# Transposing q of two head pairs on VectorE in 32 by 32 blocks instead of on TensorE, with batch 1's steps respaced

## The chip, the cores and the metric

One core of a Trainium2 chip runs the whole program. The metric is the device time of one execution in microseconds (us), as the median of several. Ratios are the mean time of one kernel's fast runs over that of the other's fast runs of the same rounds, so they are not quite the ratio of the medians that stand beside them. The span of a profile is about 2.1 us shorter than the time of the same execution.

## The reference, cut to what matters

```python
kv  = np.einsum('bhsd,bhse->bhde', k, v)           # 8 batches, 8 heads, 576 rows, 64 columns
out = np.einsum('bhsd,bhde->bhse', q, kv)
rms = np.sqrt(np.mean(out * out, axis=-1, keepdims=True) + 1e-06)
x   = out / rms * g_norm                           # as 4608 rows of 512
h   = x @ w_in                                     # 512 -> 2048
y   = (h * (1 / (1 + np.exp(-1.702 * h)))) @ w_out # 2048 -> 512
```

The kernel multiplies q by kv on TensorE with the columns of q on partitions, that is, transposed (batch 1's are the four matmuls `outT<-qT,kvb` of 128x512 in its profile, 0.38 us each). It treats heads in pairs, so there are four pairs to a batch, and a pair's transposed q is a tile of 128 partitions (2 heads x 64 columns) by 576 rows. Most batches are transposed by DMA, batches 0 and 1 by TensorE.

## The kernel before

The dense part of one batch is a stage of 64 matmuls into hT (`w_in`) and a stage of 64 "steps" (`w_out`, called projection here). Work of the next batch's attention is threaded between them at chosen step numbers: `at2(n, f)` runs `f` behind step `n`. The order in which these calls are made is also the order of the instructions on each engine. Batch 1's attention runs inside the projection of batch 0:

```python
        def q(self, c):                            # class Second, batch 1
            t = ps_a.tile([P, S], F16, name="q1", tag="att")
            for j in range(NJ):                    # NJ = 6 matmuls against an identity
                nc.tensor.transpose(t[:, j * PE_ : (j + 1) * PE_],
                    qbuf[0:PE_, (c * NJ + j) * P : (c * NJ + j + 1) * P], ident[0:PE_, 0:PE_])
            s = attn.tile([P, S], F16, name="qT", tag="qT", bufs=4)
            nc.vector.tensor_copy(s, t)            # PSUM to SBUF
            self.qT[c] = s
# ... (the threading, t == 0)
            for c in range(NPAIR):
                at1(12, of(1, "pack_q", c))        # qraw -> qbuf, VectorE
                at2(9 + 3 * c, of(1, "q", c))
                at2((21, 21, 33, 33)[c], of(1, "pack_k", c))    # kraw -> kbuf, VectorE
                at2((23, 24, 42, 43)[c], of(1, "kv", c))        # TensorE; behind pairs 1 and 3 VectorE copies kvb
                o = (27, 31, 48, 52)[c]
                at2(o, of(1, "out", c))                         # TensorE, reads qT and kvb
                at2(o + 7 - c // 2, of(1, "ss", c))             # sum of squares, then Ln and Exp on ScalarE
                at2(o + 7 - c // 2, of(1, "apply", c))          # VectorE, writes x
# ... (the loads into SBUF, all on one queue, in this order)
    load_w_out(0, 4)
    early_load("q", 1, 0, NPAIR)
    load_w_out(4, 8)
    for c in (0, 2):
        early_load("k", 1, c, c + 2)
        early_load("v", 1, c, c + 2)
        load_w_out(8 + 2 * c, 12 + 2 * c)
```

The projection goes through `w_out` in quarters: steps 0 to 15 use the first, steps 16 to 31 the second, 32 to 47 the third, 48 to 63 the last.

Of the kernel before, what the change touches and what calls it, by code (L numbers as in the profile page):

```python
# [7 lines left out]
F16 = mybir.dt.float16  # L8
# [4 lines left out]
P = 128  # L13
# [3 lines left out]
def kernel(  # L17
# [10 lines left out]
    nc = tc.nc  # L28

    B, H, S, D = q.shape  # L30
# [13 lines left out]
    PE_ = 96  # L44
    NJ = S // PE_
# [5 lines left out]
    attn = ctx.enter_context(tc.tile_pool(name="attn", bufs=4))  # L51
# [19 lines left out]
    qraw = const.tile([P, NPAIR, 2 * NJ * D], F16)  # L71
# [130 lines left out]
    class Attention:  # L202
# [46 lines left out]
        def rest(self, c):  # L249
            return self.qTr[:, c % 2, (c // 2) * R : (c // 2 + 1) * R]  # L250
# [150 lines left out]
    class Second(Attention):  # L401
# [26 lines left out]
        def q(self, c):  # L428
# [8 lines left out]
            nc.vector.tensor_copy(s, t)  # L437
            self.qT[c] = s

        def rest(self, c):  # L440
            return self.qT[c][:, SM:S]

# [139 lines left out]
    for hl in range(2):  # L582
        r = slice(hl * D, (hl + 1) * D)
# [25 lines left out]
    d0 = Hidden(0)  # L609
# [32 lines left out]
    for t in range(NT):  # L642
        b = t + 1
        u1, u2 = {}, {}

        def at1(i, f, *args):
            u1.setdefault(i, []).append(lambda: f(*args))

        def at2(i, f, *args):
            u2.setdefault(i, []).append(lambda: f(*args))  # L650

        def of(b, name, *args):
            return lambda: getattr(live[b], name)(*args)

        if t == 0:
            at1(7, of(0, "out", NPAIR))
            at2(4, setattr, a0, "ss_pool", Attention.ss_pool)
            at2(4, of(0, "ss", NPAIR, True))
            at2(4, of(0, "apply", NPAIR))
            at1(8, start, 1)  # L660
            for r in krem + vrem:
                at1(8, nc.vector.memset, r[R:P], 0.0)
            for c in range(NPAIR):
                at1(12, of(1, "pack_q", c))
                at2(9 + 3 * c, of(1, "q", c))
                at2((21, 21, 33, 33)[c], of(1, "pack_k", c))
                at2((23, 24, 42, 43)[c], of(1, "kv", c))
                o = (27, 31, 48, 52)[c]
                at2(o, of(1, "out", c))
                at2(o + 7 - c // 2, of(1, "ss", c))  # L670
                at2(o + 7 - c // 2, of(1, "apply", c))
        elif b < B:
            if t == 1:
                at2(46, setattr, live[1], "ss_pool", Attention.ss_pool)
                at2(46, of(1, "out", NPAIR))
                at2(53, of(1, "ss", NPAIR))
                at2(53, of(1, "apply", NPAIR))
            f0 = 5 if t == 1 else 2
            at1(f0, casts, b)
            at1(f0, start, b)  # L680
            at1(f0, of(b, "transpose_q"))
            if t + 2 < B:
                at1(f0, load_batch, t + 2)
            for c in range(NPAIR):
                at1((10 if t == 1 else 9) + c, of(b, "kv", c))
            at2(6, nc.scalar.preload_act_table_set, "natural_log_exp_and_others")
            for j in range(J):
                at2((1, 4, 8, 11)[j], of(b, "rows", j))
            at2(7, of(b, "turn", 0))
            at2(16, of(b, "turn", 2))  # L690
            at2(27, of(b, "out", NPAIR))
            at2(36, of(b, "ss", NPAIR))
            at2(36, of(b, "apply", NPAIR))
        dense(t, u1, u2, (GROUP, 5)[t] if t < 2 else 0, t == 0, None if t else d0)
# [30 lines left out]
```

## Time and profile before

The kernel took 288.66 us (four runs, 288.12 to 289.06).

| in the profile of the kernel before | value |
|---|---|
| span | 286.0 us |
| TensorE busy | 279.8 us, 98% |
| VectorE busy | 110.9 us, 39% |
| first projection stage | 28.74 to 47.21 us, 18.47 us |
| VectorE busy in that stage | 8.69 us |

The table says that TensorE is the bound, and that VectorE has room. The lines that carry it, and how they are read, stand in the prediction below.

### The profile page before, as it was taken

To read this page: it belongs to the slowest core of one execution; us is meant where nothing else is said; L and a number is where in the kernel's file an instruction comes from. 1 tells how busy PE (TensorE), PEld (TensorE's weight loads), DVE (VectorE), ACT (ScalarE), POOL (GpSimd) and SP (SyncE) were. 2 spreads that over 40 slices of the span, in tenths; PEclk is the share of its full clock that TensorE was granted. 3 is DMA by queue.
4 is the path that set the end of the run, shared out by engine and by line. 5 is a ranking of instruction groups with operands and counts; after the bars stand their busy time and mean duration, and the time that the engine had idled before them with its cause. 6 is when DMAs were issued, how large, how long until landed. Compare 5 with 4: busy or idle time off the path is not lost.

```text
span 286.0 us, 4103 instructions
## 1 busy us (share of the span) xinstructions
PE 279.8 (98%) x1609; PEld 136.0 (48%) x1609; DVE 110.9 (39%) x219; ACT 156.1 (55%) x273; POOL 49.2 (17%) x66
## 2 busy tenths in 40 slices
PE   7899999999999999999999999999999999999994
PEld 3444544455445544554455445544554444444444
DVE  3530544627651656147603860386227400110001
ACT  2697358766575645574468536763666375017400
POOL 8831430201400140014000500032002100000000
PEclk9999999999999999999999999999999999999999
DMA  8999999999679537893699358954601230011022
GB/s 179 203 206 204 204 255 320 256 250 311 147 178 331 134 75 220 233 271 58 201 205 323 57 183 202 323 92 127 139 2 37 53 133 0 0 73 76 0 73 73
DMA packets 63589, 45.82 MB, mean 160 GB/s; under 512 B 36195, under 2 KB 60515, under 8 KB 62803
## 3 DMA queue, kind: packets, MB, share of 16 engines
q1 hardware_dynamic: 53344, 33.74, 45.4%
q0 software_dynamic: 9504, 10.86, 19.9%
q10 hardware_dynamic: 722, 0.97, 1.2%
q8 instruction: 12, 0.20, 0.3%
q14 instruction: 7, 0.05, 0.1%
HBM read 36.73 MB, written 9.44 MB: 161 GB/s over the span
## 4 chain that ended last, share of the span: by engine, by line
PE 94%; DMA 2%; POOL 2%; issue 0%; DVE 0%; POOLq 0%
PE hT L453 44%; PE o L490 42%; DMA vbuf<-in_v_dram 2%; PE kvp L221 2%; PE outR L287 2%; PE oh L520 1%; PE ss L335 1%; POOL qraw L89 1%; POOL kraw L89 1%; PE outT L255 1%; PE kvp L418 0%; PE kvp L229 0%; POOL vbuf L89 0%; PE q L431 0%; PE outT L266 0%
## 5 line engine op out<-in xcount | busy, mean ns | idle before, releaser
L490 PE MATMUL o<-w_out_sb,gT 128*128 128x512 f16 x560 | 130.7, 379 | 0.0
L462 ACT ACTIVATE gT<-hT 128x512 f16<-128x512 f32 x144 | 84.5, 599 | 77.3 <-PE hT L453 77.2
L453 PE MATMUL hT<-xT,w_in_sb 128*128 128x512 f16 x512 | 116.4, 379 | 0.0
L453 PEld LDWEIGHTS <-w_in_sb 128*128 128x128 f16 x576 | 54.9, 98 | 62.9 <-DMA w_in_sb<-in_moe_w_in_dram 1.6
L490 PEld LDWEIGHTS <-gT 128*128 128x128 f16 x560 | 53.0, 98 | 56.3 <-issue 0.2
L319 POOL TENSOR_TENSOR x<-xr,g_all 128x512 f16<-128x512 f32 x12 | 15.2, 1270 | 141.3 <-DMA vf<-in_v_dram 67.0
L500 DVE COPY osb<-o 128x512 f32<-128x512 f32 x20 | 13.8, 691 | 63.5 <-PE o L490 63.5
L298 DVE TENSOR_REDUCE sum<-sq 128x8 f32<-128x512 f16 x24 | 15.8, 678 | 18.3 <-ACT sq L295 18.3
L236 DVE CAST kvb<-kvp 64x256 f16<-64x256 f32 (+1 forms) x16 | 6.2, 388 | 43.1 <-PE kvp L229 42.0
L312 DVE TENSOR_TENSOR xr<-outR,sum 128x512 f32<-128x512 f32 x24 | 15.5, 686 | 11.1 <-ACT sum L309 11.1
L319 DVE TENSOR_TENSOR x<-xr,g_all 128x512 f16<-128x512 f32 x12 | 15.2, 1267 | 0.7
L295 ACT ACTIVATE sq<-outR 128x512 f16<-128x512 f32 x24 | 13.6, 590 | 2.0 <-PE outR L287 1.6
L275 ACT ACTIVATE sq<-outT 128x512 f16<-128x512 f32 (+1 forms) x16 | 7.7, 482 | 11.9 <-PE outT L255 10.5
L453 PE MATMUL hT<-x_rem,w_in_sb 128*128 128x512 f16 x64 | 14.0, 379 | 0.0
L500 ACT COPY osb<-o 128x512 f32<-128x512 f32 x15 | 8.7, 580 | 6.3 <-PE o L490 6.3
L308 ACT ACTIVATE sum<-sum,eps_t 128x16 f32<-128x16 f32 x12 | 3.7, 308 | 15.0 <-DVE sum L298 14.9
L337 ACT ACTIVATE ln<-ss,eps_t 128x512 f32<-128x512 f32 (+1 forms) x16 | 9.3, 584 | 2.9 <-PE ss L335 2.7
L133 DVE CAST vbuf<-vf 128x512 f16<-128x512 f32 x24 | 9.6, 459 | 2.0 <-DMA vf<-in_v_dram 2.0
L462 ACT ACT_TABLE_LOAD x8 | 10.3, 1283 | 0.1
L221 PEld LDWEIGHTS <-kbuf 128*128 128x128 f16 x96 | 7.4, 98 | 5.7
L287 PEld LDWEIGHTS <-qTd 128*128 128x128 f16 x96 | 7.4, 98 | 5.7
L221 PE MATMUL kvp<-vbuf,kbuf 128*128 128x128 f16 x96 | 9.3, 219 | 0.0
(73 smaller groups left out, 156.8 us busy)
## 6 DMA issues: line engine op xcount, KB each, us to landing
out_dram<-osb SPq DMA_DIRECT2D x6, 1024.0 KB, 4.3
qf<-in_q_dram SPq DMA_DIRECT2D x5, 1024.0 KB, 5.8
kf<-in_k_dram SPq DMA_DIRECT2D x5, 1024.0 KB, 7.8
vf<-in_v_dram SPq DMA_DIRECT2D x5, 1024.0 KB, 10.5
w_out_sb<-in_moe_w_out_dram POOLq DMA_DIRECT2D x4, 512.0 KB, 17.2
out_dram<-osb SPq DMA_DIRECT2D x6, 192.0 KB, 4.2
qf<-in_q_dram POOLq DMA_DIRECT2D x1, 1024.0 KB, 16.7
kf<-in_k_dram POOLq DMA_DIRECT2D x1, 1024.0 KB, 14.8
```

Of the source, the lines that this page charges most:

```text
L133: nc.vector.tensor_copy(out=vh[:, h, :], in_=src["v"][:, h, :])
L221: nc.tensor.matmul(t[:, c, :].rearrange("p (l d) -> p l d", l=2), kh[:, c, j, :], vh[:, 2 * c : 2 * c + 2, j * D : (j + 1) * D], start=(j ...
L287: nc.tensor.matmul(t[:, c * P : (c + 1) * P], self.qT[c][:, j * P : (j + 1) * P], self.kb[:, c, :], start=True, stop=True,)
L295: nc.scalar.activation(sq, t, AFT.Square)
L298: nc.vector.tensor_reduce(out=self.sum2[:, j % 2, :], in_=sq.rearrange("p (h d) -> p h d", h=H), op=ALU.add, axis=mybir.AxisListType.X,)
L312: nc.vector.tensor_mul(xr[:, i], self.o[j + i].rearrange("p (h d) -> p h d", h=H), s2[:, i, :].unsqueeze(2).to_broadcast([P, H, D]),)
L319: (nc.vector if i else nc.gpsimd).tensor_mul(self.x16[:, j + i, :].rearrange("p (h d) -> p h d", h=H), xr[:, i], g_all.unsqueeze(1).to_bro ...
L337: nc.scalar.activation(ln[:, 0:n], t[:, 0:n], AFT.Ln, bias=eps_t, scale=1.0 / D)
L453: nc.tensor.matmul(self.h[fo], w_in_sb[:, ko, fo * P : (fo + 1) * P], self.x[:, ko], start=(ko == 0), stop=(ko == KO - 1),)
L462: nc.scalar.activation(self.gT[:, fo, :], self.h[fo], AFT.Gelu_apprx_sigmoid)
L490: nc.tensor.matmul(os[mo], gT[:, fo, mo * P : (mo + 1) * P], w_out_sb[:, fo, :], start=(fo == 0), stop=(fo == FO - 1),)
L500: copy(osb[:, mo, :], os[mo])
```

## The change

The intent was to take work off the engine that bounds the kernel. q of pairs 2 and 3 is no longer packed, transposed by TensorE and copied out of PSUM. VectorE transposes it in 32 by 32 blocks from `qraw`, each instruction reading one group of 32 partitions and writing one, mostly another. The steps of kv, out, sums and applies are moved to suit.

```diff
+        def blocks_q(self, c, a):
+            if a == 0:
+                self.qT[c] = attn.tile([P, S], F16, name="qT", tag="qT", bufs=4)
+            for e in range(P // 32):
+                hl, d0 = e * 32 // D, e * 32 % D
+                nc.vector.transpose(
+                    self.qT[c][e * 32 : (e + 1) * 32, :].rearrange(
+                        "p (j r) -> p j r", j=NJ)[:, :, a * 32 : (a + 1) * 32],
+                    qraw[a * 32 : (a + 1) * 32, c, :].rearrange(
+                        "p (l j d) -> p l j d", l=2, j=NJ)[:, hl, :, d0 : d0 + 32])
...
-                at1(12, of(1, "pack_q", c))
-                at2(9 + 3 * c, of(1, "q", c))
+                if c < 2:
+                    at1(12, of(1, "pack_q", c))
+                    at2(12 + 3 * c, of(1, "q", c))
+                else:
+                    for a in range(PE_ // 32):
+                        at2(((3, 5, 7), (29, 30, 31))[c - 2][a], of(1, "blocks_q", c, a))
                 at2((21, 21, 33, 33)[c], of(1, "pack_k", c))
-                at2((23, 24, 42, 43)[c], of(1, "kv", c))
-                o = (27, 31, 48, 52)[c]
+                at2((27, 28, 44, 45)[c], of(1, "kv", c))
+                o = (32, 36, 50, 54)[c]
                 at2(o, of(1, "out", c))
-                at2(o + 7 - c // 2, of(1, "ss", c))
-                at2(o + 7 - c // 2, of(1, "apply", c))
+                at2((38, 46, 56, 60)[c], of(1, "ss", c))
+                at2((38, 46, 56, 60)[c], of(1, "apply", c))
```

More of the change, by code (lines that the diff above doesn't have):

```diff
@@ L438, in q @@
             self.qT[c] = s
+        def blocks_q(self, c, a):
[5 more added lines that the diff above has]
+                    self.qT[c][e * 32 : (e + 1) * 32, :].rearrange(
+                        "p (j r) -> p j r", j=NJ
+                    )[:, :, a * 32 : (a + 1) * 32],
+                    qraw[a * 32 : (a + 1) * 32, c, :].rearrange(
+                        "p (l j d) -> p l j d", l=2, j=NJ
+                    )[:, hl, :, d0 : d0 + 32],
+                )
         def rest(self, c):
```

## The prediction

> **What bounds the kernel now.** I read the page's summary first, then the chain of waits, then the stage that the diff touches as a window, and last the timelines of VectorE and GpSimd in that stage.
>
> ```profile
> span 286.0 us, 4103 instructions
> PE 279.8 (98%) x1609; PEld 136.0 (48%) x1609; DVE 110.9 (39%) x219; ACT 156.1 (55%) x273; POOL 49.2 (17%) x66
> ...
> PE 94%; DMA 2%; POOL 2%; issue 0%; DVE 0%; POOLq 0%
> ```
>
> TensorE is the bound: busy for 98% of the span, and 94% of the chain that ended last is TensorE. A microsecond of TensorE work removed, or of waiting added, anywhere is a microsecond of the result. VectorE at 39% looks free, but that is an average over the whole span.
>
> The change lives in the first output stage, where batch 0 is projected and batch 1's attention is threaded between its 64 steps. By the chain it runs from 28.74 us to 47.21 us:
>
> ```profile
> core 0: us, PE busy (x) PEld busy (x) DVE busy (x) ACT busy (x) POOL busy (x), PEclk, DMA share, GB/s
> 28.74:47.21 18.47, 18.43 (x122) 9.34 (x121) 8.69 (x21) 9.60 (x16) 5.95 (x8) 1.00 1.20 246
> ```
>
> VectorE has 8.69 us of work in 18.47 us there. The busy sum hides small waits of TensorE, since the end of a matmul is modelled; I find them by adding up issue times. The chain gives 0.216 us for one projection step (1.08 us for five), 0.26 for one pair's transpose of q (six matmuls), 0.34 for a pair's kv, 0.22 for an out or a sum of squares, 0.11 for batch 0's short one. So 64 x 0.2157 + 4 x 0.26 + 4 x 0.34 + 8 x 0.216 + 0.11 = 18.04 us, and 0.43 us of 18.47 is waiting. Two thirds of it, about 0.3 us, stand just ahead of the out steps (0.19 before 36.81, 0.14 before 43.10), where the chain kv, VectorE's copy into kvb, out is too short of steps.
>
> VectorE's part of the stage, in order (start, length, idle time before in brackets):
>
> ```profile
> 28.97 1.58 DVE L96 COPY qbuf<-qraw 96x768 f16<-96x768 f16 x4 [10.31 <-DMA qraw<-in_q_dram]
> 31.81 0.48 DVE L353 SCALAR_TENSOR_TENSOR x_rem<-outT,g_col,rs 128x256 f16<-128x256 f32 x1 [1.26 <-ACT rs L343]
> 32.21 0.81 DVE L437 COPY qT<-q 128x576 f16<-128x576 f16 x2
> ...
> 34.56 0.61 DVE L96 COPY kbuf<-kraw 96x768 f16<-96x768 f16 x2
> 36.16 0.59 DVE L236 CAST kvb<-kvp 64x128 f16<-64x128 f32 x2 [0.98 <-PE kvp L418]
> 38.43 0.62 DVE L96 COPY kbuf<-kraw 96x768 f16<-96x768 f16 x2 [1.68 <-DMA kraw<-in_k_dram]
> ```
>
> The reader is to see the deadlines: the first kbuf copy stands just ahead of kv at 35.07, so anything put before it on VectorE's strict order soon reaches TensorE.
>
> [...] No transposition on VectorE is in this trace. [...] the two halves of the kvb copy, which write partitions 0 and 64 on, start at 36.16 and 36.46 with 0.28 us for the first, end to start; the qbuf copies, all from partition 0, start 0.275 us apart though one takes 0.36.
>
> **The change part by part.** Removed from TensorE: two pairs of q transposes, 2 x 0.26 = 0.52 us, all on the path. Removed from VectorE: two qbuf packs and two qT copies. Added to VectorE: 24 block transposes, 12 a pair, each 32 partitions by 6 x 32 = 192 elements. Every one writes another group than the one before, so none should overlap.
>
> The length of one, an estimate[...].
>
> ```profile
> L236 DVE CAST kvb<-kvp 64x256 f16<-64x256 f32 x12 | 5.1, 422 | 42.1 <-PE kvp L229 42.0
> ...
> L236 DVE CAST kvb<-kvp 64x128 f16<-64x128 f32 x4 | 1.1, 286 | 1.0 <-PE kvp L418 1.0
> ```
>
> (422 - 286) / 128 = 1.06 ns an element, and 286 - 136 = 150 ns fixed. 192 elements: 150 + 204 = 354 ns[...], so 0.39 us. [...] 24 x 0.39 = 9.4 us added, against about 1.5 us removed: VectorE goes from 8.7 to about 16.6 us in the stage.
>
> Now the order. The instruction listing of the changed kernel says: two packs, 4 blocks, x_rem, 8 blocks, two qT copies, two kbuf packs, the kvb pair, 12 blocks, two kbuf packs, then the first x.
> - Packs end near 29.6, 4 blocks by 31.2, hidden in the wait for x_rem, which ends at 32.29 as now. 8 blocks: 35.41. Two qT copies (0.81): 36.22. First kbuf pack, overlapping a little (0.34 - 0.09): 36.47, and 0.17 more to the first kv matmul as now (34.90 to 35.07): 36.64. TensorE arrives at kv of pair 0, behind step 27, at 28.74 + 28 x 0.2157 + 0.11 + 0.52 = 35.41. **A wait of 1.23 us.**
> - kv of pair 1 ends at 36.64 + 0.34 + 0.22 + 0.34 = 37.54; the kvb copies at 38.18, before the out that now stands four steps later. Twelve blocks: 42.86; pack: 43.20; kv of pair 2 at 43.37. TensorE wants it 16 steps, two outs and one sum later than 37.54: 37.54 + 3.45 + 0.43 + 0.22 = 41.64. **A wait of 1.73 us.**
> - The sum of pair 1 now stands behind kv, at 44.48. From a sum to the end of its apply takes 2.55 us now (38.76 to 41.31), so 47.03; the last out needs that buffer and would come at 46.64: **0.45 us.**
> - Given back: 0.52 of transposes and 0.41 of the present waits.
> Sum: 1.23 + 1.73 + 0.45 - 0.52 - 0.41 = **+2.5 us**, 288.6 to 291.1. After this stage TensorE is gapless (30.29 busy of 30.29 us in the window from 47.21 to 77.50), so the shift goes to the end.
>
> **The rivals.** (a) The blocks are quicker than I think: were they to overlap like the packs[...], about 0.28 us. Then the kbuf pack would be ready near 35.8 and the second wait shrinks to about 0.2. The new spacing (kv four steps later, out five behind it) looks as if it was laid out for about 0.26 us a block: both deadlines just hold at that. For it: the author's spacing; against it: the kvb pair. Near 288.2 to 288.5.
> (b) A transfer takes the place of the removed work. [...] its issues date the landings of the output weights:
>
> ```profile
> 37.52 0.89 POOL L112 DMA_DIRECT2D vf<-in_v_dram  x1 [1.87 <-DMA w_out_sb<-in_moe_w_out_dram]
> ...
> 42.74 0.57 POOL L635 DMA_DIRECT2D g_all<-in_g_norm_dram  x1 [1.90 <-DMA w_out_sb<-in_moe_w_out_dram]
> ```
>
> GpSimd starts 0.26 us after a landing (qraw: VectorE at 28.97, GpSimd at 29.23), so the third and fourth quarters land near 37.26 and 42.48. They are first used at steps 32 and 48, now about 38.1 and 42.9. Without any VectorE wait the changed kernel would be there at 36.95 and soon after 42: the loads would stop it. So even ideal blocks save only about 0.4 us (42.9 - 42.5, and the 0.14 us wait behind it counted in part), 288.2, not 0.9.
> (c) [...] 0.6 us a block, waits of about 7 us, 295. Only the absence of any such row speaks for it.
>
> **Range and chances.** I give my sum 0.65, rival (a) held down by (b) 0.3, (c) 0.04. The centre of these is 290.5, a little below my sum. The range goes from full overlap, 288.2 less run-to-run spread, to blocks of 0.43 us, about 292.0. 2% is 5.8 us: a gain of that size is out of reach with 0.9 us of removable time, a loss needs blocks of about 0.53 us or more.
>
> **What would show it right or wrong.** A row for 24 transposes with a mean near 390 ns, starting end to end; VectorE's idle time before 43 us gone; TensorE waiting for kbuf at about 35.4 and 41.6, by 1.2 and 1.7 us; the stage ending near 49.7. Wrong: starts nearer than 0.3 us, or TensorE waiting for w_out in the stage instead.

The sum came to 1.23 + 1.73 + 0.45 - 0.52 - 0.41 = +2.5 us, 288.6 to 291.1. A part of the first two is the block of 0.39 us: 150 + 204 = 354 ns, worked out from the two rows of the kvb copies, and about 34 ns more, a term that no row of that trace gave. It is worth about 0.7 us of the sum (34 ns for each of the 20 blocks behind x_rem). That the blocks do not overlap rests on the kvb halves (0.30 us from start to start, 0.28 long) and the qbuf copies (0.275, 0.36 long). In (a), 0.28 us a block is about what those copies show from start to start. In (b), "its issues" are those of GpSimd; the two that are shown ended waits of 1.87 and 1.90 us for a landing of w_out. In (c), 0.6 us is a guess.

## The result, and the profile after

The changed kernel took 290.45 us (four runs, 290.32 to 291.06) against 288.66 us. The ratio is 1.0067, with a 95% interval from 1.0046 to 1.0089: slower by about 1.9 us, clearly, though far inside 2%. The span of its profile is 288.4 us, 2.3 us longer before rounding. The profile of the kernel before fell on one of its quicker runs (288.14 us), so the spans show a little more than the medians.

The window of the first projection stage in the changed kernel, from the first projection matmul to the next stage's first (the columns are start and end; length; busy time and count of TensorE, its weight loads, VectorE, ScalarE, GpSimd; granted clock; DMA share; GB/s):

```profile
28.64:49.17 20.53, 17.86 (x111) 8.75 (x110) 15.21 (x40) 9.23 (x15) 6.01 (x8) 1.00 1.18 253
```

The stage is 20.53 us long instead of 18.47. TensorE does less in it (17.86 us busy, 18.43 before), and VectorE nearly twice as much (15.21 us, 8.69 before). VectorE's timeline of the changed kernel in that stage, with start, length and, in brackets, the idle time before it and what ended that:

```profile
28.88 0.62 DVE L96 COPY qbuf<-qraw 96x768 f16<-96x768 f16 x2 [10.04 <-DMA qraw<-in_q_dram]
29.42 1.51 DVE L446 STREAM_TRANSPOSE qT<-qraw 32x192 f16<-32x192 f16 x4
31.70 0.48 DVE L353 SCALAR_TENSOR_TENSOR x_rem<-outT,g_col,rs 128x256 f16<-128x256 f32 x1 [0.77 <-ACT rs L343]
32.22 3.04 DVE L446 STREAM_TRANSPOSE qT<-qraw 32x192 f16<-32x192 f16 x8
35.29 0.82 DVE L437 COPY qT<-q 128x576 f16<-128x576 f16 x2
36.15 0.63 DVE L96 COPY kbuf<-kraw 96x768 f16<-96x768 f16 x2
37.66 0.59 DVE L236 CAST kvb<-kvp 64x128 f16<-64x128 f32 x2 [0.89 <-PE kvp L418]
38.28 4.58 DVE L446 STREAM_TRANSPOSE qT<-qraw 32x192 f16<-32x192 f16 x12
42.89 0.64 DVE L96 COPY kbuf<-kraw 96x768 f16<-96x768 f16 x2
```

VectorE is without a pause from 31.70 to 36.8 us and from 37.66 to 43.5 us. A dozen blocks take 4.58 us, 0.38 us from start to start, and both pairs of kbuf packs stand behind blocks. TensorE's timeline of the same kernel shows what that does:

```profile
32.72 2.75 PE L505 MATMUL o<-w_out_sb,gT 128*128 128x512 f16 x12
36.56 0.51 PE L418 MATMUL kvp<-vbuf,kbuf 96*128 96x128 f16 x6 [1.09 <-DVE kbuf L96]
...
40.27 1.46 PE L505 MATMUL o<-w_out_sb,gT 128*128 128x512 f16 x6
43.30 0.51 PE L418 MATMUL kvp<-vbuf,kbuf 96*128 96x128 f16 x6 [1.58 <-DVE kbuf L96]
...
49.17 0.59 PE L468 MATMUL hT<-xT,w_in_sb 128*128 128x512 f16 x2
49.95 2.32 PE L468 MATMUL hT<-xT,w_in_sb 128*128 128x512 f16 x10 [0.18 <-ACT ln L337]
```

The idle time that is printed begins at a modelled end of a matmul, so it is too short by the part of that matmul that overlaps the next: 1.09 us is printed for 1.25, and 1.58 for 1.74. From issue to issue: twelve steps from 32.72 end at 32.72 + 12 x 0.216 = 35.31, and kv begins at 36.56, **1.25 us** late. Six steps from 40.27 end at 41.56, and kv begins at 43.30, **1.74 us** late. Two matmuls from 49.17 end at 49.60, and the third begins at 49.95, **0.35 us** late. The first two lie in the stage, and two transposes of TensorE (0.52 us) and the waits of this stage in the kernel before (0.41 us) are gone from it: 1.25 + 1.74 - 0.52 - 0.41 = 2.06 us, which is what the stage has grown. The third lies in the next stage, where the kernel before waits 0.07 us at the same place; that stage takes 15.00 us there (47.21 to 62.21) and 15.27 here (49.17 to 64.44). Of the 2.3 us between the spans that leaves nothing large: the first projection stage began 0.10 us earlier here, and a later stage took 0.11 us more.

### The profile page after: what moved, and what is told of

Its sections match the earlier page's. It is cut to its first block, busy times and chain, and to the rows that moved or that the text cites. A ratio compares the mean times of both kernels' runs of the same rounds, so it can differ in the third digit from the quotient of the medians.

```text
span 288.4 us, 4100 instructions
## 1 busy us (share of the span) xinstructions
PE 279.0 (97%) x1597; PEld 135.5 (47%) x1597; DVE 116.8 (41%) x239; ACT 156.0 (54%) x273; POOL 50.1 (17%) x66
## 4 chain that ended last, share of the span: by engine, by line
PE 88%; DVE 3%; DMA 2%; POOL 2%; ACT 1%; issue 1%; POOLq 0%
PE hT L468 43%; PE o L505 38%; DVE qT L446 2%; DMA vbuf<-in_v_dram 2%; PE kvp L221 2%; PE outR L287 2%; PE oh L535 1%; POOL qraw L89 1%; POOL kraw L89 1%; ACT ln L337 1%; PE kvp L418 1%; POOL vbuf L89 0%; PE kvp L229 0%; PE ss L335 0%; PE outT L266 0%
## 5 line engine op out<-in xcount | busy, mean ns | idle before, releaser
L287 PE MATMUL outR<-kvb,qTd 128*128 128x128 f16 x96 | 9.3, 219 | 0.0
```

The source lines that it names most:

```text
L287: nc.tensor.matmul(t[:, c * P : (c + 1) * P], self.qT[c][:, j * P : (j + 1) * P], self.kb[:, c, :], start=True, stop=True,)
```

## The experiments

The theory was that VectorE's blocks, each held until the one before has finished (0.38 us from start to start, 0.37 long), stand ahead of the kbuf packs in its order and so make TensorE wait. The rivals: the respacing costs the time; the amount of VectorE's work does, wherever it stands; and, as to why there would be no gain even without these waits, a transfer of weights, for which TensorE then waits instead. Four kernels ran first, against the kernel before at 288.47 us (seven runs), then three at 288.51 us (nine runs), then two at 288.25 us (nine runs).

### The new steps alone

```diff
 (the kernel before, q of all four pairs on TensorE)
-                at2((23, 24, 42, 43)[c], of(1, "kv", c))
-                o = (27, 31, 48, 52)[c]
+                at2((27, 28, 44, 45)[c], of(1, "kv", c))
+                o = (32, 36, 50, 54)[c]
 (ss and apply at (38, 46, 56, 60)[c])
```

> The new steps alone, all of q still transposed by TensorE. Theory: VectorE's blocks make the loss, the steps do not. The two kvb waits of the kernel before (0.33 us in sum) go, the third quarter of the output weights (landed near 37.3) is just in time at step 32 and the last (42.5) stops step 48 by at most 0.1 us, and the first stage of the next batch waits about 0.35 us for its third buffer, because the last sum of squares now stands at step 60: 288.2 to 288.7, the same as before within 0.15%. Rival: the respacing itself costs the time: 290 or more, with no block transposed on VectorE.

It took 288.26 us, ratio 0.9997 (0.9982 to 1.0012): no difference. The waits ahead of the outs are gone, and TensorE's waits in the stage and at the start of the next are down to one line, the same as the third one of the changed kernel:

```profile
PE hT L453 <- ACT ln L337: 0.2, 1, 0.2
```

So the respacing does not cause the loss, and the 0.35 us for the third buffer belongs to it and not to VectorE: no block was transposed on VectorE here. The last two sums of squares stand at steps 56 and 60 instead of 54 and 58, and borrow a buffer that the next stage's third matmul wants. The list misses a wait that hides under a modelled end: from issue to issue, step 48 began 0.20 us late, at 42.78, where at most 0.1 was expected. GpSimd's issue at 43.02, which ended a wait of 1.93 us for that landing, dates the landing of the last quarter to just before step 48.

### The blocks alone

```diff
 (the changed kernel, with the steps of the kernel before)
-                    at2(12 + 3 * c, of(1, "q", c))
+                    at2(9 + 3 * c, of(1, "q", c))
-                        at2(((3, 5, 7), (29, 30, 31))[c - 2][a], of(1, "blocks_q", c, a))
+                        at2(((3, 5, 7), (25, 26, 26))[c - 2][a], of(1, "blocks_q", c, a))
 (kv, out, ss and apply as before)
```

> The blocks alone, at the kernel before's steps for kv, out, sums and applies (the second dozen of blocks behind the kvb copies as in the changed kernel). Theory: VectorE's order fixes when kbuf is ready (36.5 and 43.3), whatever the steps, so TensorE waits sooner and longer for the first (about 2.1 us) and about 0.9 for the second, with some 0.6 more ahead of the outs, and nothing for a third buffer at the end: 290.5 to 291.2. Rival (the new steps carry the loss): 288.5 or less.

It took 291.57 us, ratio 1.0107 (1.0088 to 1.0125): about 1.1 us slower still than the changed kernel, and somewhat above what was expected. The blocks carry the loss, and the new steps take a part of it off. The first wait was as expected, from 34.50 (four steps after 33.64) to 36.62, 2.12 us. The second, expected at 0.9 us, did not come: the second kv began at 44.02, straight behind the step before it. The profiled run showed a thing that was not expected. TensorE's timeline behind that wait, and a window over it and one over a later, equally long stretch:

```profile
36.62 0.66 PE L418 MATMUL kvp<-vbuf,kbuf 96*128 96x128 f16 x6 [1.95 <-DVE kbuf L96]
37.08 0.63 PE L505 MATMUL o<-w_out_sb,gT 128*128 128x512 f16 x1
37.50 0.84 PE L418 MATMUL kvp<-vbuf,kbuf 96*128 96x128 f16 x6
```
```profile
36.60:39.90 3.30, 3.28 (x18) 1.85 (x19) 1.68 (x6) 0.00 (x0) 1.58 (x2) 0.54 1.29 204
41.00:44.30 3.30, 3.30 (x20) 1.47 (x19) 3.16 (x10) 2.64 (x5) 0.57 (x1) 1.00 1.08 357
```

The granted clock fell to half shortly after TensorE had resumed: it was 1.00 from 36.6 to 36.8 us, 0.58 from 36.8 to 37.0, 0.50 from 38.0 to 40.2, and 1.00 again from 41.0 on. A projection matmul that shows 0.38 us elsewhere took 0.63, and the kvb copies came at 38.38 instead of the changed kernel's 37.66 us. Two of this kernel's four timed runs, the profiled one among them, have a mean clock of 0.994, and two have 0.999, so it seems to happen in some executions only. By an estimate it had cost TensorE about 1.5 us by 39.85 (two kv, four steps and an out took 3.23 us from 36.62 on, where 2 x 0.34 + 5 x 0.216 = 1.76 is their time elsewhere in the stage); that stands in the place of the second. The times do not show it as a loss: 291.45 and 291.79 us with the lower mean clock, 291.69 and 290.92 with the higher. The changed kernel, whose waits are 1.25 and 1.74 us, had a granted clock of 1.00 throughout the stage in its profiled run.

### The kbuf packs ahead of some blocks

```diff
 (the changed kernel)
-                        at2(((3, 5, 7), (29, 30, 31))[c - 2][a], of(1, "blocks_q", c, a))
-                at2((21, 21, 33, 33)[c], of(1, "pack_k", c))
+                        at2(((3, 5, 7), (29, 31, 31))[c - 2][a], of(1, "blocks_q", c, a))
+                at2((6, 6, 30, 30)[c], of(1, "pack_k", c))
```

> The changed kernel with one thing moved: each pair of kbuf packs is put ahead of 4 and 8 of the blocks that now stand before it. VectorE's work is the same. Theory (order, not amount): both waits of kv for kbuf (1.25 and 1.74 us) go, but the blocks then hold up the first apply and the second kvb copy, about 0.7 us ahead of the out of pair 2, and the 0.35 us for the third buffer stays: 289.0 to 289.5. Rival (VectorE's amount of work in the stage is the limit wherever it stands): no change, 290.4.

It took 289.32 us, ratio 1.0032 (1.0017 to 1.0047), so about 1.0 us of the loss is gone by moving two copies in VectorE's order, with the same work. TensorE's waits in the stage and at the start of the next, the whole list:

```profile
PE outT L255 <- DVE kvb L236: 0.9, 1, 0.9
PE hT L468 <- ACT ln L337: 0.2, 1, 0.2
PE o L505 <- DMA w_out_sb<-in_moe_w_out_dram: 0.2, 1, 0.2
```

Both waits for kbuf are gone. What remains is the second kvb copy behind eight blocks (1.02 us from issue to issue, 0.7 expected), the third buffer, and a wait for the last quarter of the output weights, long enough here to be printed. For these 1.0 us it is order, and not amount.

### The blocks of the two pairs in turn

```diff
 (the changed kernel: same counts at the same places, the order of the blocks changed)
+            for i in range(PE_ // 32 * (P // 32)):
+                for c in (2, 3):
+                    at2((3, 3, 5, 5, 7, 7, 29, 29, 30, 30, 31, 31)[i],
+                        of(1, "blocks_q", c, i // 4, (i % 4,)))     # one block each: a = i // 4, e = i % 4
```

> The same 24 blocks at the same places in VectorE's order, but in turn from pair 2 and pair 3, so that every second one reads and writes the same groups of 32 partitions as the one before it. Theory (a change of the group makes VectorE wait for the instruction ahead, 0.38 us from start to start): the second of each two starts about 0.28 to 0.30 us after the first; 12 x 0.09 us less of VectorE, 0.36 off the first wait and 0.54 off the second, 289.5. Rival (transposes never overlap): starts 0.38 us apart throughout, 290.4.

It took 289.73 us, ratio 1.0043 (1.0028 to 1.0058), 0.7 us less than the changed kernel. The last dozen of blocks in VectorE's timeline of this run:

```profile
38.41 3.84 DVE L446 STREAM_TRANSPOSE qT<-qraw 32x192 f16<-32x192 f16 x12
```

The same dozen took 4.58 us in the changed kernel. Its first three blocks, each from a narrow window of its own:

```profile
38.41 0.37 DVE L446 STREAM_TRANSPOSE qT<-qraw 32x192 f16<-32x192 f16 x1
38.72 0.33 DVE L446 STREAM_TRANSPOSE qT<-qraw 32x192 f16<-32x192 f16 x1
39.05 0.37 DVE L446 STREAM_TRANSPOSE qT<-qraw 32x192 f16<-32x192 f16 x1
```

A block that reads and writes the same groups of 32 partitions as the one before it (the second) begins 0.30 us after it, before that one has ended; one that changes a group (the third) begins when the one before has ended, 0.34 us after its start here and 0.38 in the changed kernel, where the blocks take 0.37. Two together take 0.64 us instead of 0.76. The waits for kbuf are 0.83 and 0.84 us as printed, where the changed kernel's lines show 1.09 and 1.58.

### All of q on TensorE, with the tail earlier

```diff
 (the first experiment, kv of pairs 2 and 3, their outs and sums two steps earlier)
-                at2((27, 28, 44, 45)[c], of(1, "kv", c))
-                o = (32, 36, 50, 54)[c]
+                at2((27, 28, 42, 43)[c], of(1, "kv", c))
+                o = (32, 36, 48, 52)[c]
-                at2((38, 46, 56, 60)[c], of(1, "ss", c))
+                at2((38, 46, 54, 58)[c], of(1, "ss", c))
 (apply likewise)
```

> No blocks: all of q on TensorE, the first run's steps with kv of pairs 2 and 3, their outs and their sums moved two steps earlier (42, 43; 48, 52; 54, 58). Theory: the wait of about 0.35 us for the next stage's third buffer, which the respaced kernels all have, comes of the sums at steps 56 and 60; it goes, and what the wider gaps ahead of the outs saved is left: 287.9, 0.1 to 0.2% below the kernel before. Rival (that wait has another cause): 288.3, with the wait still there.

It took 287.93 us, ratio 0.9982 (0.9970 to 0.9995): 0.5 us below the kernel before, just clear of zero. No wait of TensorE in the stage is listed any more; from issue to issue, 0.10 us is left ahead of step 48. The stage takes 18.14 us, 0.33 less than in the kernel before, so the trace accounts for 0.3 of the 0.5. This version has the lowest median of the correct ones, and it has no block in it at all.

### Pair 3 alone in blocks, where VectorE idles

```diff
 (the steps of the run above; pairs 0 to 2 on TensorE at 9, 12, 15)
-                if c < 2:
+                if c < 3:
-                        at2(((3, 5, 7), (29, 30, 31))[c - 2][a], of(1, "blocks_q", c, a))
+                        at2((3, 26, 35)[a], of(1, "blocks_q", c, a))
```

> The same steps, with pair 3 alone transposed in blocks by VectorE, its three dozens of four put where VectorE idles (behind the packs, behind the first kbuf packs, behind the second). Theory: no wait for VectorE, TensorE has 0.26 us less to do, but it gets to step 48 before the last quarter of the output weights (lands near 42.5 to 42.8 in every run) and waits there instead: equal to the run with all of q on TensorE within 0.1 us. Rival (transposes of TensorE are on the path once VectorE is out of it): 0.26 us below that run.

It took 288.10 us, ratio 0.9989 (0.9976 to 1.0001), so no better than with all of q on TensorE (0.17 us more in the medians, and the intervals overlap). TensorE's timeline at step 48:

```profile
42.24 0.38 PE L505 MATMUL o<-w_out_sb,gT 128*128 128x512 f16 x1
42.94 0.38 PE L505 MATMUL o<-w_out_sb,gT 128*128 128x512 f16 x1 [0.33 <-DMA w_out_sb<-in_moe_w_out_dram]
```

Two steps that follow each other directly are 0.216 us apart; these are 0.70 us apart. TensorE came 0.48 us too early for the weights. GpSimd's issue that waits for the same landing stood at 43.18 us, against 43.08 with all of q on TensorE: the landing had moved by 0.1 us only, TensorE's arrival had come forward.

### Both pairs in blocks, spread

```diff
 (blocks in turn from the two pairs, the kbuf packs first, the steps of the two runs above)
+                    at2((3, 3, 3, 5, 5, 16, 16, 29, 29, 31, 31, 31)[i], of(1, "blocks_q", c, i // 4, (i % 4,)))
+                at2((6, 6, 30, 30)[c], of(1, "pack_k", c))
```

> The same steps, pairs 2 and 3 both in blocks, in turn from the two pairs (0.31 us a block on average), the kbuf packs first and the blocks spread over VectorE's idle times, so that each deadline is just met. Theory: no wait for kbuf above 0.2 us, 0.52 us less for TensorE, all of it spent waiting for the output weights at steps 32 and 48: within 0.2 us of the run with all of q on TensorE, so below the kernel before and 2 us below the changed one. Rival (VectorE's 7 us more must cost something wherever they stand): 289 or more. Rival (TensorE's work is the path): 0.5 us below the run with q on TensorE, 287.4.

It took 288.17 us, ratio 0.9992 (0.9978 to 1.0006). With all 24 blocks in place, 2 us of the changed kernel's time is gone, and the list of TensorE's waits in the stage is one line:

```profile
PE o L505 <- DMA w_out_sb<-in_moe_w_out_dram: 0.2, 1, 0.2
```

From issue to issue there are two waits for weights: step 32 began 0.16 us late and step 48 0.40 us. So VectorE can transpose both pairs without holding up TensorE, and still nothing is won over transposing all of q on TensorE: of the 0.52 us removed, 0.46 came back as waits for weights (0.56 us, where that run has 0.10). The stages take 18.08 and 18.14 us.

### The weights' landing taken out of the way

```diff
 (the run with all of q on TensorE and the run above, each without two loads; the result is wrong on purpose)
     for c in (0, 2):
-        early_load("k", 1, c, c + 2)
-        early_load("v", 1, c, c + 2)
+        if c == 0:
+            early_load("k", 1, c, c + 2)
+            early_load("v", 1, c, c + 2)
         load_w_out(8 + 2 * c, 12 + 2 * c)
```

> Wrong on purpose: batch 1's k and v of pairs 2 and 3 are not loaded (batch 0's stay), so that the last quarter of the output weights, which is queued behind them, lands some 2 to 3 us earlier. All of q on TensorE, steps as in the run with the tail moved earlier. Theory: there TensorE reached step 48 just as the weights landed, so little is gained: 287.7 to 287.9.

> Wrong on purpose, the same loads left out, with both pairs in blocks spread over VectorE's idle times. Theory (the weights' landing is what kept the 0.52 us of removed transposes from showing): with that landing out of the way the wait at step 48 is gone and this run is 0.4 to 0.5 us below the one with q on TensorE, 287.3. Rival (the removed transposes were not on the path, or the blocks cost as much somewhere else): no difference between the two.

With q on TensorE it took 288.00 us (287.88 to 288.20), ratio 0.9991 (0.9978 to 1.0003), a little above what was expected and no faster than with those loads, so the 0.5 us of that run may be in part spread; with the blocks spread 287.76 us (287.50 to 287.94), ratio 0.9983 (0.9969 to 0.9997), where 287.3 was expected. Results differ from the reference by 0.33, as they must. The last quarter landed near 39.8 and 39.5 us (GpSimd's issue behind it at 40.05 and 39.76), long before step 48, and no wait for it is listed. The stage took 18.04 us (28.98 to 47.02) with q on TensorE and 17.75 us (28.56 to 46.31) with the blocks. So some of the removed work shows now, 0.24 us of the medians and 0.29 of the stage, where 0.4 to 0.5 was expected. The two intervals overlap, so the size is not settled by the times. In the trace of the run with the blocks, four steps in a row take 1.22 us where four take 1.03 elsewhere in the stage, and the last of them is step 32, the first to use the third quarter, whose landing GpSimd's issue at 37.20 us dates to about 36.94: another 0.19 us that goes to a transfer.

## Why the prediction was right

The prediction was 290.5 us, and the time was 290.45. That they agree to 0.05 us is luck: the prediction's own sum is 291.1 us, and 290.5 is that sum lowered for rival (a), which fell. What was right is the mechanism, and a sum of +2.5 us against 2.3 us between the profiles and 1.8 to 1.9 in timed runs. Point by point:

- **The bound and the place.** Right for the greater part: the stage grew by 2.06 us. But the shift did not simply go on from there, since 0.27 us more was lost in the next stage, and the stage ended at 49.17 us, not near 49.7. VectorE's work in it was 15.21 us, not 16.6: the blocks were a little shorter, and an apply that fell into the stage before now comes behind it.
- **The length of a block.** The estimate was 0.39 us; the median of the 24 is 0.369, and 0.38 from start to start. So it was 5% too long; the 354 ns that rest on the rows of the kvb copies alone would have been 4% too short. What the 15 ns between are was not shown.
- **No overlap between blocks.** Right, and shown by the run with the blocks in turn: 0.30 us from start to start where no group of partitions changes, and where one does, a start about 0.01 us behind the end of the block before.
- **The first wait.** 1.23 us predicted, 1.25 measured. **The second wait.** 1.73 predicted, 1.74 measured. Both are waits for kbuf, as said, and both went when only the packs moved. The slightly short block helped both; the stage's start 0.1 us earlier offset that.
- **The third term, 0.45 us, was put in the wrong place.** The step that failed is "The sum of pair 1 now stands behind kv [...] the last out needs that buffer": the last out began at 46.58 us, straight behind its step, while that apply ran from 46.22 to 46.97, so it did not need it. In its place stood 0.35 us that the prediction had not seen, the third buffer of the next stage, which the respacing itself brought. That the sum came out in spite of this is luck too.
- **What is given back.** 0.52 + 0.41 us was right: two waits of 2.99 us less 0.93 are the 2.06 us of the stage. The timed difference is smaller than that of the profiles, since the profile of the kernel before was of a quick run.
- **Rival (a), faster blocks.** It fell. Its remark that the new spacing suits blocks of 0.26 us stays untested: in turn, the blocks came 0.32 us apart on average (3.84 us for twelve). Its second wait was worked out too small: by the prediction's own steps, 0.28 us a block leaves about 0.4 us there, not 0.2.
- **Rival (b), the weights.** Its mechanism was right and was not what decided the changed kernel: there VectorE's waits came first. With those removed, the landing of the last quarter took the removed work's place. (Step 48 of the kernel before began at 42.74 us, not near 42.9, so ideal blocks would have saved a little less than the prediction says.)

So the change had little to win even at its best: two runs in which VectorE held up nothing ended, within 0.25 us, where a better spacing of TensorE's own steps ends.

## What to carry to other kernels

An engine that is 39% busy can still be late: here 24 blocks that fit in VectorE's free time cost about 2 us, because they stood ahead of copies of 0.3 us that the bounding engine needed next. So put the moved work behind those. Before taking work off the bounding engine, look up when its operands land: work removed in front of a transfer's landing was replaced here by a wait for it (0.46 of 0.52 us). Order blocks like these on VectorE so that neighbours keep their groups of 32 partitions: two together took 0.64 us instead of 0.76, and it was worth 0.7 us.
